# Sums of w_out's pieces by accumulating transfers, and a set of differences on GpSimd in place of VectorE

## The chip, the cores and the metric

The kernel runs on one core of one Trainium2 chip. The metric is the device time of one execution in microseconds; the time before is the median of three runs. The profiled execution is one more run of the same program. Engines are named as in the profile: PE (TensorE matmul), PEld (its weight loads), DVE (VectorE), ACT (ScalarE), POOL (GpSimd), SP (SyncE).

## The reference

Two blocks follow one another: a chunked state-space scan (mamba2 SSD) over x (4, 8, 768, 32), a, B and C, and a feed-forward layer with ELU on its result.

```python
for c in range(nc):                       # chunks of 32
    L = np.exp(cum[:, :, :, None] - cum[:, :, None, :]) * causal
    M = np.einsum('bhin,bhjn->bhij', Cc, Bc) * L
    y[:, :, sl] = M @ xc + (Cc @ state) * exp(cum)
    state = decay_full * state + sum_j(Bx * decay_from_j)
x = y.transpose(0, 2, 1, 3).reshape(B * S, H * D)      # (3072, 256)
h = x @ w_in                                           # (3072, 2048)
g = np.where(h > 0, h, np.exp(np.minimum(h, 0)) - 1)
out = g @ w_out                                        # (3072, 256)
```

All inputs and the output are float32, as the kernel sees them; the weights come as pairs of 32-bit words that the kernel first puts together.

## The kernel before, in words

The 3072 tokens are 12 blocks of 256, taken two at a time; a pair is named by its first block n = 0, 2, 4, 6, 8, 10. Each pair passes through the scan (`scores`, `sums`, `weigh`, `states`, `across`, `inside`), the first layer and the second layer. The order of the instructions of every engine is the order in which the program issues them (`tc.manual_schedule()`): no planner moves anything, and an engine that waits holds up all that stands behind it. The scan of pair n + 2 is woven into the first layer of pair n, and the second layer of pair n - 2 too.

**First layer.** For the columns m = 8 to 15 of pair 2 and for all columns of later pairs (m = 0 to 15, 128 columns each), `l1_words` splits each product into three passes of word products on PE (L791): the high words `w1` with `y1`, the low words `w0` with `y0`, and `both`. It needs, of the weights' piece i = m // 2, the tile `w_words` (`words_of_w`: an ACT copy L740 and a DVE operation L741) and the low words (`low_of_w`: two differences on POOL, shown at L851, because `sub` is there). After the products come ACT L799, DVE L802, ACT L808 and L809 (`begin_end`), then DVE L816 (`end_words`), which for even m is followed by a difference on POOL (L851 g<-g). `both_of_y` and `words_of_y` (L763, L766, L776) prepare the words of y for the next pair; PE needs them at the start of that pair's stage.

**Second layer.** For the first pair it is `l2`, direct products with `w_out` (L835). For later pairs `second` does it by blocks in seven products instead of eight (L910, a form of Strassen's): the weight matrix is cut in four, `a_out` = a11, a12, a21, a22, each 128 partitions x 8 x 128 as a strided view of `w_out`, and products r = 0 to 6 use a11, a12, s1, s2, s3, a22, s4. These sums of the weights are

- s3 = a11 - a21 (`s_out[1]`), s1 = a21 + a22 (over a21 itself), s2 = s1 - a11 (`s_out[0]`), s4 = a12 - s2 (`s_out[2]`).

They are made once, in 8 slices of 128x128. `differences` (POOL, L851 w_sum<-w_out) makes s3, since s1 overwrites a21. `sum_weights` (POOL, L718, three operations for each slice) makes s1, s2, s4 for slices 0 to 5 in the iterations j = 8 to 13, each after the last direct product that reads that slice of a21. The six operations for slices 6 and 7 (`left`) are handed to DVE, two in each of the iterations k = 2, 3, 4 of pair 4's stage. On the side of g, `quarters` gives b11, b21, b12, b22; `sum_t1` forms b12 - b11 and `sum_t2` forms t from b22 - b12. `sum_t1` of pair 2 is issued with `nc.vector` (DVE, L864), four times, at i = j - 8 = 0, 1, 3, 4.

Products and adds of the second layer alternate between two pools of PSUM: `ps_o` of even numbers comes from a pool with one buffer, so a product r + 2 waits until the adds of product r (DVE L888, ACT L922 and L947) have read it.

**Queues around the change.** Loads are issued by SP. POOL issues no transfer. On POOL, in j = 7, stand the two selects of a decay (L530), the low words of piece 5, then the scaling of B for blocks 4 and 5 (L412), then the weight sums. On ACT, in j = 6 and 7, stand the exponentials of the decays (L525), the copy of block 0's result (L841) and `elu`.

Of the kernel before, what the change touches and what calls it, by code (L numbers as in the profile page):

```python
# [14 lines left out]
ALU = mybir.AluOpType  # L15
ACT = mybir.ActivationFunctionType
# [16 lines left out]
def kernel(  # L33
# [27 lines left out]
    nc = tc.nc  # L61
# [30 lines left out]
    for k in range(4):  # L92
        (nc.scalar if k % 2 else nc.sync).dma_start(
            out=la0[BH * k:BH * (k + 1)],
            in_=a.rearrange("b h (c s) -> (b h) c s", s=P)[:, 0:2, :])
# [187 lines left out]
    for v in range(2):  # L283
        nc.gpsimd.affine_select(
            out=low16[Q * v:Q * v + Q], in_=low16[Q * v:Q * v + Q], pattern=[[1, Q]],
# [5 lines left out]
        out=hmask, in_=hmask, pattern=[[-N, NH]], compare_op=ALU.is_ge, fill=0.0,  # L291
        base=0, channel_multiplier=1)
    nc.gpsimd.affine_select(
        out=hmask, in_=hmask, pattern=[[N, NH]], compare_op=ALU.is_ge, fill=0.0,
# [8 lines left out]
        out=minus, in0=ident, scalar1=-1.0, scalar2=None, op0=ALU.mult)  # L303
# [213 lines left out]
    def decay(n, q):  # L517

        decay_of(n, 2 * q)
        decay_of(n, 2 * q + 1)  # L520
# [185 lines left out]

    def sum_weights(eng, a, s, i):
        for step in weight_steps(eng, a, s, i):  # L710
            step()

    def weight_steps(eng, a, s, i):
        a11, a12, a21, a22 = (part[:, i] for part in a)
        s2, _, s4 = (part[:, i] for part in s)
        for out, in0, in1, op in (
                (a21, a21, a22, ALU.add), (s2, a21, a11, ALU.subtract), (s4, a12, s2, ALU.subtract)):
            yield lambda: eng.tensor_tensor(out=out, in0=in0, in1=in1, op=op)  # L718

    def weight_sums():  # L720
        return [conv.tile([P, MC // 2, P], F32, tag="w64", name="w_sum", bufs=W_AHEAD)
                for _ in range(3)]

    w_parts = w_out.rearrange("p (i k) (r c) -> p k r i c", k=2, c=P)
    a_out = [w_parts[:, k, r] for r in range(2) for k in range(2)]
    s_out = []
# [8 lines left out]
    def words_of_w(i):  # L735

        w = pieces[i][0]
        k_words[i] = conv.tile(
            [P, 2, KC, CW], F32R, tag="w64", name="w_words", bufs=W_AHEAD)
        nc.scalar.activation(k_words[i][:, 0], w, ACT.Copy, scale=NEAR)  # L740
        nc.vector.scalar_tensor_tensor(  # L741
            out=k_words[i][:, 1], in0=k_words[i][:, 0].bitcast(F32), scalar=1.0 / WORD - 1.0,
            in1=w, op0=ALU.mult, op1=ALU.add)

    def low_of_w(i):

        w0 = conv.tile([P, KC, CW], F32R, tag="w_in", name="w0", bufs=DF // CW + 1)
        for k in range(KC):
            sub(w0[:, k], pieces[i][0][:, k], k_words[i][:, 0, k].bitcast(F32))
        k_words[i] = k_words[i], w0  # L750
# [99 lines left out]
    def sub(out, in0, in1):  # L850
        nc.gpsimd.tensor_tensor(out=out, in0=in0, in1=in1, op=ALU.subtract)  # L851

    def quarters(n, i):


        if n == 2 and i < DIRECT:
            A, B = g_of[n, i], g_of[n + 1, i]
            return A[:, 0], A[:, 1], B[:, 0], B[:, 1]
        A, B = g_of[n, 2 * i], g_of[n, 2 * i + 1]
        return A[:, 0], B[:, 0], A[:, 1], B[:, 1]  # L860

    def sum_t1(n, i, eng=nc.gpsimd):
        b11, b21, b12, b22 = quarters(n, i)
        eng.tensor_tensor(out=b12, in0=b12, in1=b11, op=ALU.subtract)  # L864
# [107 lines left out]
    def w_take(i, low):  # L972

        w_abs(i)
        w_low(i, low)
        w_sign(i)

    def w_give(i):

        w_high(i)  # L980
        w_sum(i)
# [190 lines left out]
            at = k // 2 * 2 + late  # L1172
            turn_part(*[(m, 0), (m, 1), (m, 2), (m + 1, 0), (m + 1, 1), (m + 1, 2), (m, 3), (m + 1, 3)][at])

    def differences(i, count):
        for r in range(i, i + count):
            sub(s_out[1][:, r], a_out[0][:, r], a_out[2][:, r])

    for j in range(2 * DIRECT):
        n, i = 2 + j // DIRECT, j % DIRECT  # L1180
        if j < 7:
            l2(0, j)
        piece = todo < len(pieces) and j != 1
        if j == 0:
            elu()
        if piece:
            w_take(todo, nc.vector)
        l1(n, i)
        if j == 7:
            l2(0, j)  # L1190
        if j == 0:
            scaled(3, nc.gpsimd)
            turn(3)
            elu()
            turn_exp(3)
        if piece:
            w_give(todo)
            todo += 1
        while lag:
            elu()  # L1200
        if j == 4:
            w_take(todo, nc.scalar)
            w_give(todo)
            todo += 1
        if j == 0:
            decay(3, 2)
            decay(3, 3)
        if j == 1:
            scores(3)
            sums(3)  # L1210
            for q in range(4):
                weigh(3, q)
        if j == 2:
            states(3)
        if j == 3:
            inside(across(3), 3)
        if j == 4:
            words_of_y(2)
        if j == 4:
            words_of_w(4)  # L1220
        if j == 5:
            low_of_w(4)
        if j == 5:
            both_of_y(2)
        scan_ahead(j)
        if j == 3:
            s_out[:] = weight_sums()
        if j == 7:
            words_of_w(5)
            low_of_w(5)  # L1230
    for j in range(8, 16):
        i = j - 8
        l1_words(2, j, between=4 if i == 7 else None)
        for p in ((), (6,), (), (7,), (0,), (1,), (2,), ())[i]:
            words_of_w(p)
        for p in ((), (), (6,), (7,), (0,), (), (), ())[i]:
            low_of_w(p)
        if i == 7:
            l2(1, 6)
            l2(1, 7)  # L1240
        begin_end()
        if i == 0:
            turn_part(5, 2)
            scaled(4, nc.gpsimd)
            scaled(5, nc.gpsimd)
        if i < 2:
            load_bc(i + 6)
            l2(1, i)
        if i == 2:
            l2(1, 2, half=0)  # L1250
            scores(4, 5)
            sums(4, 5)
            for q in range(4):
                weigh_two(4, q)
            l2(1, 2, half=1)
            states(4)
            states(5)
            turn_part(4, 3)
            turn_part(5, 3)
            for to in (6, 7):  # L1260
                load_b(to)
                spread_cum(to)
        if i == 3:
            l2(1, 3)
        if i == 4:
            y = across(4, 5)
            inside(y, 4, 5, ts=(0,))
            l2(1, 4)
        if i == 5:
            l2(1, 5, half=0)  # L1270
            inside(y, 4, 5, ts=(1,))
            l2(1, 5, half=1)
        if i in (0, 1, 3, 4):
            sum_t1(2, (0, 1, 3, 4).index(i), nc.vector)
        if i in (4, 6):
            turn_part(6, i // 2 - 2)
        if i in (0, 2, 3, 5):
            differences((0, 0, 2, 4, 0, 6)[i], 2)
        if i < 6:
            sum_weights(nc.gpsimd, a_out, s_out, i)  # L1280
    end_words()
    for p in (1, 2):
        low_of_w(p)
# [2 lines left out]
    low_of_w(3)  # L1286
    sum_t2(2, 0)
    sub(g_of[2, 14][:, 1], g_of[2, 14][:, 1], g_of[2, 14][:, 0])
    left = (step for i in (6, 7) for step in weight_steps(nc.vector, a_out, s_out, i))

    def stage_scan(n, k):

# [19 lines left out]
    for n in range(4, NP, 2):  # L1312
        m = n + 2 if n + 2 < NP else None
        steps = second(n - 2)

        def l2s(count):
            for _ in range(count):
                next(steps)

        for k in range(16):  # L1320
            l1_words(n, k, between=m if k == 15 else None)
            turn_step(n, k // 2 * 2 + 1, k % 2)
            if n == 4 and k == 0:
                decay(6, 1)
            if n == 4 and 1 < k < 5:
                for _ in range(2):
                    next(left)()
            if m:
                stage_scan(n, k)
            begin_end()  # L1330
            if k == 0 and n > 4:
                store(n - 4, 0)
                store(n - 4, 1)
            if not m:
                l2s(4 if k % 2 else 3)
                continue
            l2s((3 + (n == 4), 3 - (n == 4), 3, 3, 3, 3, 3, 3, 4, 5, 2, 2, 3, 1, 1, 0)[k])
            if k == 9:
                scores(m, m + 1)
                sums(m, m + 1)  # L1340
                for q in range(4):
                    weigh_two(m, q)
                l2s(2)
                states(m)
            if k == 10:
                states(m + 1)
            if k == 13:
                y = across(m, m + 1)
                inside(y, m, m + 1, ts=(0,))
                l2s(4)  # L1350
                inside(y, m, m + 1, ts=(1,))
        if m:
            l2s(4)
            both_of_y(m)
        end_words()
        for _ in steps:
            pass
    n = NP - 2
# [34 lines left out]
```

## Time and profile before

| | |
|---|---|
| median of 3 runs | 350.58 us (350.37 to 350.59) |
| profiled execution | 350.72 us |
| its span | 348.8 us |
| granted clock of TensorE | 0.999 |
| busy share PE, PEld, DVE, ACT, POOL | 98%, 86%, 74%, 67%, 63% |
| POOL: 18 sums L718 | 3.6 + 3.4 + 3.1 us |
| POOL: 8 differences w_sum L851 | 4.3 us |
| DVE: 6 sums L718 | 0.30 to 0.81 us each, 125.7 to 133.1 us |
| DVE: 4 first sums of t, L864 | 0.68 to 0.96 us each, 88.0 to 104.1 us |

How to read it: times inside the span are in microseconds from its start. A line such as "L910 PE MATMUL ps_o<-w_out,g 128*128 128x128" gives the source line, the engine, the operation, and what is written from what; "x4" counts instructions; a bracket with an arrow gives the idle time of the engine before the instruction and what ended it. Matmuls are pipelined, so a busy PE is not PE at its peak.

### The profile page before, as it was taken

Reading aid. Unit: us, or ns where it says so; the run is one execution under the profiler, and the core shown is the slowest. Engines: PE = TensorE matmul, PEld = TensorE weight load, DVE = VectorE, ACT = ScalarE, POOL = GpSimd, SP = SyncE. Lnnn points to the kernel's source line nnn. Section 1 sums busy time; section 2 is a strip of 40 time slices with the busy share of each in tenths; the row PEclk is TensorE's granted clock in tenths of the full one; section 3 lists DMA queues with packets and bytes.
Section 4 is the critical chain, followed back from the end, with each engine's and each line's share of the span. In section 5 each row is a group of like instructions: output and inputs, shape, how many; then the busy total and the mean of one; then the engine's idle time right before and its main releaser. Section 6 shows DMA issues by size and latency. Waiting matters only on the chain.

```text
span 348.8 us, 9876 instructions
## 1 busy us (share of the span) xinstructions
PE 340.7 (98%) x3878; PEld 298.3 (86%) x3878; DVE 258.5 (74%) x514; ACT 235.2 (67%) x538; POOL 219.4 (63%) x338
## 2 busy tenths in 40 slices
PE   8999999999999999999999999999999999999996
PEld 5669888888878788888999988998988999999996
DVE  3998989879987799875878775888675756665232
ACT  4789989599748789647699447699557566665000
POOL 5554554558999998964196864196854174455860
PEclk9999999999999999999999999999999999999999
DMA  8988988551360601080431070320000100001002
GB/s 148 238 217 181 309 187 226 123 93 43 65 137 2 131 22 31 7 156 12 103 64 32 8 158 6 95 44 2 2 0 5 62 0 3 0 0 43 22 0 62
DMA packets 72727, 26.49 MB, mean 76 GB/s; under 512 B 57768, under 2 KB 67560, under 8 KB 72680
## 3 DMA queue, kind: packets, MB, share of 16 engines
q1 hardware_dynamic: 70360, 25.60, 31.6%
q8 instruction: 30, 0.49, 0.6%
q10 hardware_dynamic: 2320, 0.26, 0.5%
q14 instruction: 17, 0.14, 0.1%
HBM read 22.51 MB, written 3.34 MB: 74 GB/s over the span
## 4 chain that ended last, share of the span: by engine, by line
PE 80%; DVE 7%; ACT 6%; SPq 2%; DMA 2%; issue 2%; POOL 0%; DVEq 0%; ACTq 0%; POOLq 0%
PE ps_o L910 32%; PE ps_h L791 16%; PE ps_h L671 11%; PE ps_w L791 8%; PE ps_o L835 6%; PE ps_y L638 2%; DVE ps_h L802 2%; DMA w<-in_moe_w_in_dram 2%; ACT e L809 1%; ACT e L808 1%; PE ps_g L545 1%; PE ps_y L620 1%; PE ps_st L575 1%; ACT e L799 1%; ACT L L525 1%
## 5 line engine op out<-in xcount | busy, mean ns | idle before, releaser
L910 PEld LDWEIGHTS ps_o<-w_out,g 128*128 128x128 f32 x640 | 78.6, 191 | 3.6 <-ACT p_sum L922 0.2
L910 PE MATMUL ps_o<-w_out,g 128*128 128x128 f32 x640 | 80.3, 275 | 0.0
L808 ACT ACTIVATE e<-ps_h 128x512 f32<-128x512 f32 x72 | 43.0, 597 | 53.5 <-DVE ps_h L802 53.5
L816 DVE SCALAR_TENSOR_TENSOR g<-e,ps_h 128x512 f32<-128x512 f32 x72 | 49.3, 685 | 30.6 <-ACT e L809 30.1
L851 POOL TENSOR_TENSOR g<-g 128x256 f32<-128x256 f32 x36 | 27.2, 757 | 57.2 <-DVE g L816 56.9
L802 DVE SCALAR_TENSOR_TENSOR ps_h<-ps_h,e 128x512 f32<-128x512 f32 x72 | 50.0, 695 | 13.9 <-ACT e L799 11.3
L799 ACT ACTIVATE e<-ps_w 128x512 f32<-128x512 f32 x72 | 42.2, 586 | 14.4 <-PE ps_w L791 14.3
L791 PE MATMUL ps_w<-y_both,w_words 128*128 128x512 f32 x144 | 51.2, 435 | 0.5 <-DVE y_both L776 0.4
L809 ACT ACTIVATE e<-e 128x512 f32<-128x512 f32 x72 | 45.5, 632 | 2.3
L671 PE MATMUL ps_h<-yT,w_in 128*128 128x256 f32 (+1 forms) x208 | 45.2, 368 | 1.3 <-POOL w_in L252 1.3
L791 PE MATMUL ps_h<-y,w_words 128*128 128x512 f32 x144 | 46.1, 401 | 0.1
L791 PE MATMUL ps_h<-y,w 128*128 128x512 f32 x144 | 44.6, 391 | 0.0
L671 PEld LDWEIGHTS ps_h<-yT,w_in 128*128 128x128 f32 x208 | 36.3, 190 | 7.4 <-POOL w_in L252 2.6
L525 ACT ACTIVATE L<-L,ncum 128x64 f32<-128x64 f32 x160 | 42.2, 336 | 0.2
L910 PE MATMUL ps_o<-w_sum,g 128*128 128x128 f32 x304 | 38.5, 275 | 0.9 <-DVE p_sum L888 0.7
L910 PEld LDWEIGHTS ps_o<-w_sum,g 128*128 128x128 f32 x304 | 37.0, 192 | 2.5 <-POOL g L851 0.9
L530 POOL TENSOR_SCALAR_AFFINE_SELECT L<-L 64x512 f32<-64x512 f32 x40 | 29.6, 741 | 11.0 <-ACT L L525 9.7
L791 PEld LDWEIGHTS ps_h<-y,w 128*128 128x128 f32 x144 | 27.0, 188 | 6.4
L851 POOL TENSOR_TENSOR g<-t,g 128x256 f32<-128x256 f32 x40 | 28.1, 736 | 5.8 <-PE ps_o L910 5.7
L791 PEld LDWEIGHTS ps_h<-y,w_words 128*128 128x128 f32 x144 | 26.5, 188 | 5.9 <-PE ps_w L791 0.5
L835 PE MATMUL ps_o<-w_out,g 128*128 128x256 f32 x128 | 30.9, 383 | 0.0
L851 POOL TENSOR_TENSOR t<-g 128x256 f32<-128x256 f32 x40 | 29.1, 759 | 0.3
(134 smaller groups left out, 540.4 us busy)
## 6 DMA issues: line engine op xcount, KB each, us to landing
L<-flat SPq DMA_DIRECT2D x20, 256.0 KB
w<-in_moe_w_out_dram SPq DMA_DIRECT2D x8, 512.0 KB
w<-in_moe_w_in_dram SPq DMA_DIRECT2D x7, 512.0 KB
xr<-in_x_dram SPq DMA_DIRECT2D x24, 128.0 KB
out_dram<-c_sum SPq DMA_DIRECT2D x9, 256.0 KB
bc<-in_B_dram SPq DMA_DIRECT2D x24, 64.0 KB
bc<-in_C_dram SPq DMA_DIRECT2D x22, 64.0 KB
ec<-flat_exp SPq DMA_DIRECT2D x10, 128.0 KB
```

The source lines that it names most:

```text
L525: nc.scalar.activation(L[:, h, u], L[:, h, u], ACT.Exp, bias=ncum[:, u, row:row + 1])
L530: nc.gpsimd.affine_select(out=part, in_=part, pattern=[[0, 4], [0, 2], [1, Q]], compare_op=ALU.is_ge, fill=0.0, base=0, channel_multiplier=-1)
L671: nc.tensor.matmul(out=ps[:, j, toks], lhsT=w_in[i][:, k, j * P:(j + 1) * P], rhs=yT[n // 2][:, k, n % 2].rearrange("p u i -> p (u i)")[:, ...
L791: nc.tensor.matmul(out=ps, lhsT=lhs[:, k], rhs=rhs[:, k], start=k == 0 and lhs is not w0, stop=k == KC - 1 and lhs is not w1)
L799: nc.scalar.activation(e, both, ACT.Copy, scale=WORD)
L802: nc.vector.scalar_tensor_tensor(out=high, in0=high, scalar=WORD - 1.0, in1=e, op0=ALU.mult, op1=ALU.add)
L808: nc.scalar.activation(e, high, ACT.Relu, scale=-1.0)
L809: nc.scalar.activation(e, e, ACT.Exp, scale=-1.0)
L816: nc.vector.scalar_tensor_tensor(out=g_of[n, m].rearrange("p b i -> p (b i)"), in0=e, scalar=1.0, in1=h, op0=ALU.subtract, op1=ALU.max)
L835: nc.tensor.matmul(out=o_of[n][:, ts], lhsT=g_of[n, j][:, m % 2, ts * P:(ts + 1) * P], rhs=w_out[:, m], start=(m == 0 and ts == 0), stop=( ...
L851: nc.gpsimd.tensor_tensor(out=out, in0=in0, in1=in1, op=ALU.subtract)
L910: nc.tensor.matmul(out=ps[:, ts], lhsT=b[:, ts * P:(ts + 1) * P], rhs=a[:, i], start=(i == chunk[0] and ts == 0), stop=(i == chunk[-1]), s ...
```

## The change

All sums of the weights are now made of negating copies on ACT (`less`) and transfers that add the source to what stands in the destination (`plus`, issued from POOL's queue): s3 = -a21, then + a11; s2 = -s3, then + a22; s4 = -s2, then + a12; and a21 + a22 in place, in two halves. Each step reads the one before, so ACT waits for the transfers and POOL for ACT. `less` of s3 stands in j = 6 behind the decay's exponentials, its `plus` in j = 7 ahead of the low words of piece 5. `less` of s2 is at the end of i = 2 (after `begin_end` of m = 10), its `plus` in i = 3, `less` of s4 in i = 5 behind the copies to yT, its `plus` in i = 6. The first half of a21 + a22 is issued in i = 5, the second after `sum_t2(2, 0)`. The six operations on DVE in pair 4's stage are gone. `sum_t1` of pair 2 is issued from POOL.

```diff
-    def sum_weights(eng, a, s, i):
...
-        for out, in0, in1, op in (
-                (a21, a21, a22, ALU.add), (s2, a21, a11, ALU.subtract), (s4, a12, s2, ALU.subtract)):
-            yield lambda: eng.tensor_tensor(out=out, in0=in0, in1=in1, op=op)
+    def less(out, in_):
+        nc.scalar.activation(out, in_, ACT.Copy, scale=-1.0)
+    def plus(out, in_, rows=slice(None)):
+        nc.gpsimd.dma_start(out=out[:, rows], in_=in_[:, rows], accum_op=ALU.add)
...
-    def differences(i, count):
-        for r in range(i, i + count):
-            sub(s_out[1][:, r], a_out[0][:, r], a_out[2][:, r])
...
+        if j == 6:
+            less(s_out[1], a_out[2])
         if j == 7:
             words_of_w(5)
+            plus(s_out[1], a_out[0])
             low_of_w(5)
...
         if i in (0, 1, 3, 4):
-            sum_t1(2, (0, 1, 3, 4).index(i), nc.vector)
+            sum_t1(2, (0, 1, 3, 4).index(i))
...
-        if i in (0, 2, 3, 5):
-            differences((0, 0, 2, 4, 0, 6)[i], 2)
-        if i < 6:
-            sum_weights(nc.gpsimd, a_out, s_out, i)
+        if i == 2:
+            less(s_out[0], s_out[1])
+        if i == 3:
+            plus(s_out[0], a_out[3])
+        if i == 5:
+            less(s_out[2], s_out[0])
+            plus(a_out[2], a_out[3], slice(0, 4))
+        if i == 6:
+            plus(s_out[2], a_out[1])
...
     sum_t2(2, 0)
     sub(g_of[2, 14][:, 1], g_of[2, 14][:, 1], g_of[2, 14][:, 0])
-    left = (step for i in (6, 7) for step in weight_steps(nc.vector, a_out, s_out, i))
+    plus(a_out[2], a_out[3], slice(4, 8))
...
-            if n == 4 and 1 < k < 5:
-                for _ in range(2):
-                    next(left)()
```

More of the change, by code (lines that the diff above doesn't have):

```diff
@@ L695, in elu @@
             op0=ALU.subtract, op1=ALU.max)
-    def sum_weights(eng, a, s, i):
[L710 to L715, printed above, removed]
-        for out, in0, in1, op in (
-                (a21, a21, a22, ALU.add), (s2, a21, a11, ALU.subtract), (s4, a12, s2, ALU.subtract)):
-            yield lambda: eng.tensor_tensor(out=out, in0=in0, in1=in1, op=op)
+    def less(out, in_):
+        nc.scalar.activation(out, in_, ACT.Copy, scale=-1.0)
+    def plus(out, in_, rows=slice(None)):
+        nc.gpsimd.dma_start(out=out[:, rows], in_=in_[:, rows], accum_op=ALU.add)
     def weight_sums():
```

## The prediction

> **What bounds the kernel now.** I read the busy shares first, then the table of stretches, the waits of the matmul engine, and at last the engines' timelines around the edited lines. A profiled execution took 350.72 us, of which the span is 348.8; the median of the three timed runs, 350.58, is 0.14 below it, so I build the sum on the profiled one and take 0.14 off.
>
> ```profile
> PE 340.7 (98%) x3878; PEld 298.3 (86%) x3878; DVE 258.5 (74%) x514; ACT 235.2 (67%) x538; POOL 219.4 (63%) x338
> ```
>
> PE has 8 us of idle in the whole span. The change touches 80 to 160 us. Columns of the stretches: window, length, then busy time of PE, PEld, DVE, ACT, POOL.
>
> ```profile
> 80.00:100.00 20.00, 19.56 (x251) 16.16 (x250) 18.84 (x39) 12.71 (x30) 18.51 (x31) 1.00 0.38 80
> 100.00:120.00 20.00, 19.50 (x234) 16.19 (x224) 15.89 (x24) 15.33 (x34) 19.22 (x28) 1.00 0.30 74
> 120.00:140.00 20.00, 19.13 (x124) 16.74 (x124) 18.55 (x33) 17.69 (x47) 18.42 (x26) 1.00 0.14 35
> 140.00:160.00 20.00, 19.43 (x347) 17.33 (x346) 15.41 (x37) 11.92 (x24) 14.20 (x26) 1.00 0.40 74
> 180.00:200.00 20.00, 20.00 (x256) 18.22 (x254) 15.41 (x32) 15.84 (x41) 15.59 (x23) 1.00 0.06 18
> ```
>
> Here POOL is busy 18 to 19 of 20 us and DVE up to 18.8, more than anywhere after; PE loses 2.4 us in the four stretches and nothing in the undisturbed one below. The waits of PE say on whom:
>
> ```profile
> PE ps_o L910 <- DVE p_sum L888: 0.7, 1, 0.7
> PE ps_st L575 <- DVE c_sum L888: 0.6, 1, 0.6
> PE ps_y L620 <- DVE g L816: 0.4, 1, 0.4
> PE ps_w L791 <- DVE y_both L776: 0.4, 1, 0.4
> PE ps_o L910 <- ACT c_sum L947: 0.2, 1, 0.2
> ```
>
> So PE is the bound, and behind it the DVE-ACT chain is just too late at five places. Idle is not all: the stage of pair 4 is also stretched where PE counts as busy. From the chain of waits, the third word product of a stage (k = 2) to its last (k = 15), first for pair 4, then for pair 6:
>
> ```profile
> 120.20 0.93 PE ps_h L791 x4
> 163.80 0.92 PE ps_h L791 x4
> 174.64 0.91 PE ps_h L791 x4
> 216.37 0.92 PE ps_h L791 x4
> ```
>
> 43.60 us against 41.73 for the same products: 1.87 us lost in the stage that holds the sums left to DVE. That is the most this stage can give back.
>
> **What the change removes.** POOL loses 8 differences (L851 w_sum, 4.3 us) and 18 sums (L718: 3.6 + 3.4 + 3.1), together 14.4 us between 91 and 116. DVE loses six sums in the stage of pair 4 (L718, 0.76 + 0.81 + 0.67 + 0.71 + 0.30 + 0.72 = 3.97 us, 125.7 to 133.1) and four first sums of t (L864, 0.95 + 0.85 + 0.68 + 0.96 = 3.44 us, 88.0 to 104.1).
>
> - In the stage of pair 4, the add for which PE waits runs at 130.10 behind 2.6 us of these sums; without them it is done before PE asks. I give the whole 1.87 back: **-1.87**.
> - The wait at L620 (0.44): DVE reaches that L816 at 98.68. Without two of the first sums (1.80 us before that point) and with POOL's Sx no longer held up (DVE stood 0.82 us on it at 96.75), it comes about 1 us earlier: **-0.44**.
>
> **What it adds.** Three negating copies of 128x1024 on ACT; by L922 (128x256, 0.35) and L799 (128x512, 0.59) each is 0.59 + 2 x 0.25 = 1.1 us. Four first sums of t on POOL, 4 x 0.76 = 3.0 us, in the place of 14.4. Five accumulating transfers, four issued where POOL's program still has work behind them that PE needs, three of 512 KB and two of half that. The trace has no transfer issued by POOL, so the time that an issue holds POOL (call it X) must be bounded.
>
> - Below: a load of SP's queue with as many pieces as ours (xr, 128 partitions x 8 heads, so 1024 runs) holds SP 0.47 to 0.58 us. Nothing lets it be below that, for it must write at least as many addresses.
> - Above: POOL summed the same 1024 runs in eight instructions of about 0.52 us, 4.2 us.
> - I take X = 3.0: it is POOL that works through the 1024 runs, as in its own row, while SP's row is that of a queue which computes nothing; nearer to POOL's.
>
> The first transfer is the one without cover. It stands in POOL's program behind the two selects of block 5's decay and ahead of the low words of piece 5, which PE uses in the third product of m = 10:
>
> ```profile
> 85.68 1.72 POOL L530 TENSOR_SCALAR_AFFINE_SELECT L<-L 64x512 f32<-64x512 f32 x2 [0.90 <-ACT L L525]
> 87.48 2.06 POOL L851 TENSOR_TENSOR w<-w_in,w_words 128x256 fp32r<-128x256 f32 x2
> 89.51 1.72 POOL L412 TENSOR_TENSOR b_tok<-b_tok,eb 128x256 f32<-128x256 f32 x2
> ```
> ```profile
> 89.39 0.63 PE L791 MATMUL ps_h<-y,w_words 128*128 128x512 f32 x2
> 89.86 0.62 PE L791 MATMUL ps_h<-y,w 128*128 128x512 f32 x2
> ```
>
> The low words end at 89.54; PE needs their second half at about 90.0. The cover is 0.5 us. The selects wait for ACT, where the first negation (1.1 us, less 0.17 of idle ahead of L841) now stands before the decay: they start at 86.6 and end near 88.2. Then X, then the two subtractions (1.4 to 2.06 us as here): they end at 89.6 + X to 90.3 + X. PE stands still for X - 0.4 to X + 0.3, about X - 0.1: **+2.9**. Behind them on POOL are b_tok (needed by PE at 92.40, L575; PE is late by then too, so nothing), one first sum, the difference of g for m = 8, and the next low words (needed at 103.7, covered by over 8 us).
>
> The second negation waits on ACT for the first transfer; ACT then sits idle for 4.18 us until 99.99 in the old trace, so it costs nothing unless the transfer lands more than 4 us late. Behind it on ACT stands L799 of m = 11.
>
> The second transfer is issued when POOL has done the difference of m = 10 (DVE's L816 near 98.4, counted without PE's stall), two low words and a first sum: from 101.3 to 104.3. The third negation, on ACT between the yT copies and L799 of m = 14, waits for its landing:
>
> ```profile
> 107.46 1.13 ACT L655 COPY yT<-ps_y 128x256 f32<-128x256 f32 x3
> 108.61 0.60 ACT L799 ACTIVATE e<-ps_w 128x512 f32<-128x512 f32 x1
> ```
>
> ACT, no longer behind DVE, ends the copies at 107.15. The last 64 KB store is issued by 346.6 and the span ends at 348.8, so a landing takes some 2.2 us; 512 KB at the page's highest rate (309 GB/s) take 1.7 us, twice that if the destination is read first, and all of it may pass during the issue. The landing is between 106.5 and 109.9; I take 108.0, 0.85 late. From there ACT's L759, DVE's L766 and L776 lead straight to PE's wait at 115.17. A punctual third negation would bring L759 to 110.8 instead of 111.14 (-0.35); 0.85 late makes it **+0.5**.
>
> The third and fourth transfers wait for PE (reads of the old piece, 106.7) and for ACT's third negation. Behind them are the low words of pieces 1 to 3, from 117.8 needed by PE one after the other; POOL has 14.4 - 3.0 = 11.4 us less to do there, which hides 1.5 X = 4.5. The fifth, half as large, holds the selects and the differences g<-t: their first is done at 126.3 today and used at 130.66, so about 2 us of cover after the 0.7 that PE wins; nothing at X/2 = 1.5, a wait beyond X = 4. PE's reads of the sums (from 123.9 on) come over 10 us after their issues.
>
> Sum: 2.9 - 1.87 - 0.44 + 0.5 = **+1.1 us**, 351.8 for a profiled execution, **351.7** for the median. Its own range is 351.3 (X = 2.6) to 354.0 (X = 4.2 and the second transfer 2 us late).
>
> **Rivals.**
>
> - *A short issue: faster.* If POOL's issue is like SP's, X = 0.6 to 1.2, the low words cost PE 0.5 to 1.1, the second transfer lands before 107, and the sum is 0.8 - 1.87 - 0.44 - 0.35 = -1.9: **348.7**. It decides below X = 2. For it: every row of a DMA issue in this trace without a full queue is under 0.6 us. Against it: none of those rows is POOL's. The Trainium skill, page "DMA: Bandwidth & Descriptors", section "Latency and other measured facts", puts the first byte of a transfer issued by GpSimd at about 1 us, the emission by its cores included, against 0.6 us for the other queues. By that figure X is 1 and the sum, as an estimate from that page, -1.8; no run shown here has such a transfer.
> - *Late landings: much slower.* The accumulation reads two operands for each one written, in runs of 512 bytes. If it lands 5 us after my 108.0, ACT waits as long and PE follows through y_both: +1.1 + 4 to 5, **356**. Against it: 512 KB of loads go by at over 200 GB/s in the first quarter.
> - *Even.* X near 2.4 with a punctual second transfer: 2.3 - 2.66 = -0.4, **350.2**. That the sums simply stay on POOL is no case: the program has five copies in their place.
>
> **Chances.** About 0.2%, 0.7 us, is what a measurement of this kernel can tell from no change. Forecast 0.39, late landings 0.10: slower 0.49. Short issue 0.39: faster. Even 0.12. The range takes the short issue down to X = 1 and the forecast up to the start of the late landings: 348.8 to 354.8; about 0.18 lies outside.
>
> **What would show it.** A gap of PE, some 3 us long at L791 of m = 10 with POOL's low words as its releaser, shows the first step; a gap of 1 us or less there means a short issue. The stage of pair 4 from k = 2 to k = 15 should take 41.7 us and its waits on L888 be gone; if it stays over 43, the gain was not DVE's sums. An idle ACT ahead of the third negation, released by a transfer, shows the second cost. I am wrong if POOL passes the first transfer in 1 us, or if PE idles for a transfer in the product with the sums.

## The result

The changed kernel takes 352.90 us, the median of 6 runs (352.18 to 354.42); the kernel before took 350.48 beside it (6 runs). The ratio is 1.0069, 95% interval 1.0046 to 1.0093: slower by 2.4 us. The profiled execution took 352.93 us, with a span of 351.0 and a granted clock of 0.995. Line numbers of the changed kernel, from the edited lines on, are those of before less 3 (L791 is now L788, L851 is L848, L816 is L813, L799 is L796); those ahead of them (L530, L575, L620) are the same. The negating copies are L711, the transfers L715.

### The profile page after: what moved, and what is told of

It reads as the page before. It is cut to its first block, busy times and chain, and to the rows that moved or that the text cites. A ratio compares the mean times of both kernels' runs of the same rounds, so it can differ in the third digit from the quotient of the medians.

```text
span 351.0 us, 9859 instructions
## 1 busy us (share of the span) xinstructions
PE 342.2 (97%) x3878; PEld 299.3 (85%) x3878; DVE 253.6 (72%) x504; ACT 237.7 (68%) x541; POOL 215.7 (61%) x321
## 4 chain that ended last, share of the span: by engine, by line
PE 84%; ACT 6%; DVE 2%; SPq 2%; DMA 2%; issue 1%; POOL 1%; ACTq 0%; POOLq 0%
PE ps_o L907 36%; PE ps_h L788 18%; PE ps_w L788 9%; PE ps_h L671 9%; PE ps_o L832 5%; PE ps_y L638 2%; ACT L L525 2%; DMA w<-in_moe_w_in_dram 2%; PE ps_g L545 2%; PE ps_y L620 1%; PE ps_st L575 1%; ACT e L684 1%; SPq L179 1%; DVE y L763 1%; ACT e L691 1%
## 5 line engine op out<-in xcount | busy, mean ns | idle before, releaser
L907 PEld LDWEIGHTS ps_o<-w_out,g 128*128 128x128 f32 x640 | 79.7, 194 | 3.4
L907 PE MATMUL ps_o<-w_out,g 128*128 128x128 f32 x640 | 81.3, 278 | 0.0
L813 DVE SCALAR_TENSOR_TENSOR g<-e,ps_h 128x512 f32<-128x512 f32 x72 | 49.3, 685 | 35.4 <-ACT e L806 35.0
L848 POOL TENSOR_TENSOR g<-g 128x256 f32<-128x256 f32 x36 | 27.4, 761 | 57.0 <-DVE g L813 56.6
L799 DVE SCALAR_TENSOR_TENSOR ps_h<-ps_h,e 128x512 f32<-128x512 f32 x72 | 50.0, 695 | 15.2 <-ACT e L796 12.6
L788 PE MATMUL ps_w<-y_both,w_words 128*128 128x512 f32 x144 | 51.8, 439 | 0.7 <-DVE y_both L773 0.6
L796 ACT ACTIVATE e<-ps_w 128x512 f32<-128x512 f32 x72 | 42.2, 586 | 13.7 <-PE ps_w L788 13.6
L671 PE MATMUL ps_h<-yT,w_in 128*128 128x256 f32 (+1 forms) x208 | 45.2, 368 | 1.9 <-POOL w_in L252 1.9
L788 PE MATMUL ps_h<-y,w 128*128 128x512 f32 x144 | 45.2, 393 | 1.7 <-DVE y L763 1.1
L788 PE MATMUL ps_h<-y,w_words 128*128 128x512 f32 x144 | 45.8, 399 | 0.1
L671 PEld LDWEIGHTS ps_h<-yT,w_in 128*128 128x128 f32 x208 | 36.3, 190 | 8.1 <-POOL w_in L252 3.4
L530 POOL TENSOR_SCALAR_AFFINE_SELECT L<-L 64x512 f32<-64x512 f32 x40 | 30.7, 767 | 10.6 <-ACT L L525 8.3
L788 PEld LDWEIGHTS ps_h<-y,w 128*128 128x128 f32 x144 | 27.0, 188 | 9.1 <-POOL w L848 3.1
L788 PEld LDWEIGHTS ps_h<-y,w_words 128*128 128x128 f32 x144 | 26.5, 189 | 6.1 <-ACT y L756 0.4
L848 POOL TENSOR_TENSOR g<-t,g 128x256 f32<-128x256 f32 x40 | 28.0, 734 | 5.8 <-PE ps_o L907 5.7
L848 POOL TENSOR_TENSOR t<-g 128x256 f32<-128x256 f32 x40 | 29.1, 757 | 0.3
```

What stands on the lines that cost most here:

```text
L530: nc.gpsimd.affine_select(out=part, in_=part, pattern=[[0, 4], [0, 2], [1, Q]], compare_op=ALU.is_ge, fill=0.0, base=0, channel_multiplier=-1)
L671: nc.tensor.matmul(out=ps[:, j, toks], lhsT=w_in[i][:, k, j * P:(j + 1) * P], rhs=yT[n // 2][:, k, n % 2].rearrange("p u i -> p (u i)")[:, ...
L788: nc.tensor.matmul(out=ps, lhsT=lhs[:, k], rhs=rhs[:, k], start=k == 0 and lhs is not w0, stop=k == KC - 1 and lhs is not w1)
L796: nc.scalar.activation(e, both, ACT.Copy, scale=WORD)
L799: nc.vector.scalar_tensor_tensor(out=high, in0=high, scalar=WORD - 1.0, in1=e, op0=ALU.mult, op1=ALU.add)
L813: nc.vector.scalar_tensor_tensor(out=g_of[n, m].rearrange("p b i -> p (b i)"), in0=e, scalar=1.0, in1=h, op0=ALU.subtract, op1=ALU.max)
```

## The profile after

The busy shares of the kernel after:

```profile
PE 342.2 (97%) x3878; PEld 299.3 (85%) x3878; DVE 253.6 (72%) x504; ACT 237.7 (68%) x541; POOL 215.7 (61%) x321
```

DVE and POOL both have less to do, as intended, and PE's busy time went up by 1.5 us for the same 3878 products. The stretches of the kernel after (window, length, busy time of PE, PEld, DVE, ACT, POOL, granted clock, DMA share, GB/s) show where:

```profile
80.00:100.00 20.00, 19.41 (x189) 15.49 (x188) 17.57 (x35) 15.24 (x35) 17.05 (x24) 1.00 0.51 94
100.00:120.00 20.00, 18.17 (x259) 13.93 (x258) 15.09 (x21) 12.77 (x25) 15.14 (x15) 0.99 0.90 134
120.00:140.00 20.00, 20.00 (x125) 18.17 (x125) 14.25 (x24) 18.67 (x50) 17.92 (x24) 0.93 0.35 63
140.00:160.00 20.00, 20.00 (x251) 18.02 (x249) 16.27 (x39) 12.36 (x26) 16.73 (x29) 1.00 0.37 72
```

In the second stretch PE is idle for 1.8 us, though no other engine is busy for more than 15.2 of 20; in the two after it it is never idle, but in the third the granted clock is 0.93. The waits of PE in the whole span without those of its start (L267 and L671), in total, number and longest:

```profile
PE ps_h L788 <- DVE y L763: 1.1, 2, 0.7
PE ps_h L788 <- POOL w L848: 0.6, 2, 0.4
PE ps_w L788 <- DVE y_both L773: 0.6, 1, 0.6
```

The waits on c_sum and p_sum in pair 4's stage are gone, and so is the one at L620. In their place are one of 0.6 us for POOL, and 1.7 us for the words of y, in the first column of pair 4.

Columns are followed best by their first product of the high words (`ps_h<-y,w_words` in PE's timeline; in most columns the two products of `both` stand ahead of it). That of m = 8 comes before PE meets anything that the edit changes, and lies between 82.0 and 84.1 us from one execution to the next. The table gives the start of each column's first such product after that point, in us, in each profiled execution. The kernels e1 to e9 are described below.

| | m=10 | m=11 | m=12 | m=14 | k=0 | k=1 | k=15 |
|---|---|---|---|---|---|---|---|
| before | 6.87 | 11.98 | 15.08 | 24.81 | 30.38 | 35.24 | 81.04 |
| after | 7.16 | 13.37 | 16.48 | 25.53 | 31.52 | 39.62 | 82.99 |
| e1 | 7.13 | 12.37 | 16.68 | 25.84 | 31.77 | 38.26 | 83.23 |
| e2 | 7.16 | 13.38 | 16.84 | 25.99 | 31.55 | 35.36 | 80.29 |
| e3 | 7.17 | 12.42 | 16.15 | 25.30 | 30.86 | 34.67 | 79.32 |
| e4 | 6.87 | 11.97 | 15.08 | 25.78 | 31.34 | 36.18 | 81.74 |
| e5 | 7.06 | 13.27 | 16.39 | 25.47 | 31.52 | 36.98 | 82.42 |
| e6 | 7.05 | 13.28 | 16.40 | 25.43 | 31.99 | 38.48 | 83.41 |
| e7 | 6.87 | 11.98 | 15.10 | 24.82 | 30.38 | 35.25 | 80.36 |
| e8 | 7.12 | 12.58 | 15.75 | 24.81 | 30.37 | 34.47 | 79.78 |
| e9 | 7.16 | 12.63 | 15.82 | 24.87 | 30.43 | 35.37 | 80.40 |

After against before, piece by piece: +0.3 to m = 10, +1.1 from m = 10 to 11, -0.7 from m = 12 to 14, +0.4 to k = 0, **+3.2 from k = 0 to 1**, and -2.4 in the rest of the stage; together +1.95 at k = 15. The first 0.3 arise ahead of m = 9. ACT's copy of block 0's result (L838) stands behind the first negation and ends at 84.96, and PE's next direct products start at 85.01; before, that copy ended at 83.49 and the products started at 84.09. The trace lists no wait there, and no run tests this cause.

**The first transfer.** All five transfers of the kernel after, then POOL's timeline around the first and PE's at m = 10 (start, length, engine, line, operation; the bracket is the idle time before and what ended it):

```profile
L715 POOL DMA_DIRECT2D w_sum<-w_out x3: 1544/1550/1768, 88.8 to 111.6; - x3
L715 POOL DMA_DIRECT2D w_out<-w_out x2: 1273/1848/2424, 107.5 to 127.6; - x2
DMA to landing us min/median/max: 4.2/6.4/8.9
```
```profile
87.13 1.72 POOL L530 TENSOR_SCALAR_AFFINE_SELECT L<-L 64x512 f32<-64x512 f32 x2 [1.57 <-ACT L L525]
88.81 1.77 POOL L715 DMA_DIRECT2D w_sum<-w_out  x1
90.65 1.42 POOL L848 TENSOR_TENSOR w<-w_in,w_words 128x256 fp32r<-128x256 f32 x2
```
```profile
90.42 0.63 PE L788 MATMUL ps_h<-y,w_words 128*128 128x512 f32 x2
91.43 0.49 PE L788 MATMUL ps_h<-y,w 128*128 128x512 f32 x1 [0.38 <-POOL w L848]
92.12 0.50 PE L788 MATMUL ps_h<-y,w 128*128 128x512 f32 x1 [0.20 <-POOL w L848]
```

An issue of 512 KB (the three that write w_sum) holds POOL for 1.5 to 1.8 us, and over all five transfers the data have landed 4 to 9 us after the issue. PE's two gaps are 0.6 us of waiting; with the slower start of each product the column loses 1.1.

**The second transfer and the third negation.** ACT's negations s2 and s4 in the kernel after, then DVE's preparation of the words of y and POOL beside it:

```profile
97.77 1.06 ACT L711 ACTIVATE w_sum<-w_sum 128x1024 f32<-128x1024 f32 x1 [2.29 <-DMA w_sum<-w_out]
110.21 1.06 ACT L711 ACTIVATE w_sum<-w_sum 128x1024 f32<-128x1024 f32 x1 [0.49 <-DMA w_sum<-w_out]
```
```profile
112.39 1.36 DVE L738 SCALAR_TENSOR_TENSOR w_words<-w_words,w_in 128x512 fp32r<-128x512 f32 x1
114.73 2.16 DVE L763 SCALAR_TENSOR_TENSOR y<-y,yT 128x512 fp32r<-128x512 f32 x2
116.82 1.81 DVE L773 SCALAR_TENSOR_TENSOR y_both<-y,yT 128x512 fp32r<-128x512 f32 x2
```
```profile
111.57 1.55 POOL L715 DMA_DIRECT2D w_sum<-w_out  x1 [1.69 <-ACT w_sum L711]
112.49 5.00 POOL L848 TENSOR_TENSOR w<-w_in,w_words 128x256 fp32r<-128x256 f32 x4
```

Two things stand in one chain. ACT waits 0.49 us for the second transfer and then negates for 1.06, ahead of L796 of m = 14 and of its own copy for y. And POOL, idle for 1.69 us because the fourth transfer has to wait for that negation, does the low words of pieces 1 and 2 only afterwards, just when DVE makes the words of y: DVE's L763 takes 2.16 us for two, its L773 1.81.

**The clock.** The two-microsecond stretches of the kernel after, with the granted clock third from the end:

```profile
114.00:116.00 2.00, 1.51 (x7) 0.71 (x5) 1.90 (x4) 1.34 (x3) 1.92 (x3) 1.00 1.31 144
116.00:118.00 2.00, 0.85 (x2) 0.25 (x2) 2.00 (x3) 0.00 (x0) 1.48 (x2) 1.00 1.24 198
118.00:120.00 2.00, 1.81 (x9) 1.46 (x10) 1.84 (x4) 0.13 (x1) 0.00 (x0) 0.87 0.76 198
120.00:122.00 2.00, 2.00 (x12) 2.00 (x11) 0.84 (x2) 1.97 (x5) 0.22 (x1) 0.50 1.01 164
122.00:124.00 2.00, 2.00 (x10) 1.65 (x9) 1.34 (x3) 2.00 (x9) 2.00 (x3) 0.78 0.49 79
```

PE was busy for 2.4 of the 4 us from 114 to 118. Then the granted clock reads 0.50 for a whole stretch and 0.87 and 0.78 in its neighbours, while PE shows no idle time from 120 us on. These two are means: with finer stretches the clock is 0.50 from 119.5 to 122.8 and 1.00 up to 119.4 and from 122.9. All six runs of the kernel after have a mean clock of 0.990 to 0.995. The Trainium skill, page "TensorE: Matmul & The Clock Gate", section "What's actually happening", has the clock go to half after an idle window of about 3.4 us that runs freely. The trace agrees in the half clock, but not in the idle window: PE was busy for 59% of the 4 us ahead.

**The stage of pair 4**, k = 2 and k = 15, in the chain of waits of the kernel after:

```profile
125.32 0.91 PE ps_h L788 x4
166.50 0.92 PE ps_h L788 x4
```

It takes 41.18 us, even less than the 41.73 forecast. The experiments show that the change's own gain here is smaller.

## The experiments

The first four kernels ran on one chip beside a median of 350.98 for before (31 runs), e5 to e8 on another beside 350.93 (31 runs), e9 beside 350.57 (17 runs). Each number is a median of 10 runs, 12 for e9. The theory at the start: the loss is made of PE's stall at m = 10 and of the late words of y, the first worth about 1 us and the second 2 to 3. The rival: the stall alone carries it, as the prediction had it.

**e1_low_words_first**: the first transfer goes behind the low words of piece 5.

```diff
             words_of_w(5)
-            plus(s_out[1], a_out[0])
             low_of_w(5)
+            plus(s_out[1], a_out[0])
```

> The first transfer issued behind the low words of piece 5 instead of ahead of them. Theory (the cost lies in where the issues and negations stand): PE's wait for POOL at m = 10, 1.1 us with the clock of the traces, goes, and nothing else: 351.8 us against 352.9 of the changed kernel. Rival A (the cost is the traffic of the transfers themselves, or the program as a whole): unchanged, 352.9.

Measured: 353.65 us, ratio 1.0069 (1.0047 to 1.0091), no gain at all; its profiled execution, at 352.02, is the fastest of its ten. The stall did go (m = 11 at 12.37 instead of 13.37), but at m = 12 nothing of it is left. A line of ACT's timeline and one of PE's waits in e1:

```profile
97.20 1.06 ACT L711 ACTIVATE w_sum<-w_sum 128x1024 f32<-128x1024 f32 x1 [2.88 <-DMA w_sum<-w_out]
```
```profile
PE ps_h L788 <- ACT e L796: 1.0, 1, 1.0
```

The first transfer now lands later, the second negation waits for it longer, and L796 of m = 11, behind it on ACT, keeps PE waiting for 1.0 us. So PE's wait for POOL hid a second wait of the same length.

**e2_s4_late**: the third negation moves behind the last direct products, past the words of y, and its transfer behind the low words of pieces 1 and 2.

```diff
             l2(1, 7)
+            less(s_out[2], s_out[0])
...
         if i == 5:
-            less(s_out[2], s_out[0])
             plus(a_out[2], a_out[3], slice(0, 4))
-        if i == 6:
-            plus(s_out[2], a_out[1])
...
     for p in (1, 2):
         low_of_w(p)
+    plus(s_out[2], a_out[1])
```

> The third negation on ACT moved out of the chain that makes the words of y for pair 4, to behind the copy of block 1's result, and its transfer behind the low words of pieces 1 and 2. Theory: the words of y come 1.1 to 1.5 us earlier, PE's idle ahead of pair 4's stage falls from about 3 us to 1 or less, and TensorE's granted clock stays at 1.00 between 118 and 124, which is worth 1.6 us more: 349.9 us, between 349.4 and 350.6. Rival B (the words of y are late because POOL's low words of pieces 1 and 2 now run beside DVE's operations on y and slow them down): the wait stays above 2 us and the clock still drops: 352 or more. Rival A: unchanged.

Measured: 350.07 us, ratio 0.9966 (0.9946 to 0.9986): 0.9 us below before, and 3.6 below after by the two ratios to before (0.0103 of 350.5). From k = 0 to 1 it needs 3.81 us instead of 8.10, and PE does not wait for the words of y. This is where the time had gone.

**e3_both_moves**: e1 and e2 together.

> Both moves. Theory: the gains add, 352.9 - 1.1 - 3.0 = 348.8 us, faster than the kernel before by some 1.7. Rival A: 352.9. Rival B: 351.8.

Measured: 349.51 us, ratio 0.9956 (0.9936 to 0.9975). The first move is worth 0.6 us on top of e2, half of what was expected, and the intervals overlap.

**e4_t_on_gpsimd_only**: the kernel before with only the second part of the change.

```diff
-            sum_t1(2, (0, 1, 3, 4).index(i), nc.vector)
+            sum_t1(2, (0, 1, 3, 4).index(i))
```

> The kernel before with the four first sums of t on POOL instead of DVE and nothing else changed. Theory: DVE is freed of 3.4 us between 88 and 104, but POOL, busy 92 to 96 per cent there, gets 3.0 us more and hands over its low words later: within 0.7 of 350.5 to slower by 1, and PE's wait at L620 (0.44) gets no shorter. Rival: that move alone is the gain, 349.8.

Measured: 352.16 us, ratio 1.0038 (1.0017 to 1.0060). By itself the move of the first sums of t costs 1.2 us. The waits of PE in e4:

```profile
PE ps_y L620 <- POOL Sx L597: 0.6, 1, 0.6
PE ps_y L620 <- DVE g L816: 0.4, 1, 0.4
```

With the sums of the weights still on POOL, its Sx comes too late, and the wait for DVE stays beside it.

**e5_s4_transfer_late_only**: of e2, only the transfer moves; the negation stays in i = 5.

```diff
-        if i == 6:
-            plus(s_out[2], a_out[1])
...
     for p in (1, 2):
         low_of_w(p)
+    plus(s_out[2], a_out[1])
```

> The changed kernel with the fourth transfer (s4 + a12) issued behind POOL's low words of pieces 1 and 2; the third negation stays on ACT where the change has it. POOL then makes those low words some 3 us earlier and no longer beside DVE's operations on y (L763, L773). Theory C (two causes of about equal size: ACT is 1.1 us late, and POOL's work beside DVE costs another 1.2): y_both comes 1.2 us earlier, PE's idle ahead of pair 4's stage is about half, the granted clock stays at 1.00: 351.0, between 350.5 and 351.6. Rival (ACT's lateness alone): no change in the wait, 352.5 to 353.5. Rival (POOL's work alone): as good as e2, 350.1.

Measured: 351.71 us, ratio 1.0022 (0.9996 to 1.0048), between after and e2. DVE and POOL in e5:

```profile
113.48 1.64 DVE L763 SCALAR_TENSOR_TENSOR y<-y,yT 128x512 fp32r<-128x512 f32 x2
115.04 1.28 DVE L773 SCALAR_TENSOR_TENSOR y_both<-y,yT 128x512 fp32r<-128x512 f32 x2
```
```profile
111.82 2.14 POOL L848 TENSOR_TENSOR w<-w_in,w_words 128x256 fp32r<-128x256 f32 x2 [2.35 <-issue]
113.91 1.56 POOL L715 DMA_DIRECT2D w_sum<-w_out  x1
```

Counted from m = 8, DVE's L773 is done at 32.59 in before (115.11), 35.37 in after (118.63), 34.32 in e5 (116.32) and 32.53 in e2 (115.49). So of 2.8 us, 1.05 go when POOL's low words move away from DVE, and 1.8 come with the negation in ACT's chain (in the latter 0.35 of the same contention, for e2's L763 pair takes 1.29 us and that of e5, beside a last subtraction, 1.64). The split is rough, for the negation waits 1.26 us for its transfer in e5 and 0.49 in after. The trace of after gives much the same: counted from m = 8, ACT's copy for y (L756) starts 1.80 us later than in before, and the other 0.98 are added behind it.

DVE's four operations take 2.92 us here, 3.97 in after and 2.58 in e2, where POOL is idle beside them. POOL works on a transfer's issue (113.91 to 115.47) beside the end of the L763 pair and the start of the L773 pair, which is not stretched; its subtractions do stretch them. So did the sums of the weights that POOL made there in the kernel before:

```profile
111.78 1.61 DVE L766 SCALAR_TENSOR_TENSOR y<-y,yT 128x512 fp32r<-128x512 f32 x2
113.31 1.80 DVE L776 SCALAR_TENSOR_TENSOR y_both<-y,yT 128x512 fp32r<-128x512 f32 x2
```

These make 3.41 us. The change thus did not bring this contention; it put other work of POOL's in the same place. The Trainium skill, page "SBUF — State Buffer", section "Who interferes with whom", says that a DVE instruction with two inputs in SBUF contends with one of GpSimd that reads SBUF. The trace agrees: the L773 pair takes 1.81 us beside subtractions in after and 1.29 beside an idle POOL in e2.

**e6_pe_kept_busy**: ten more products in PE's waits at the head of pair 4's stage, to tell the clock from the waits.

```diff
+            if (n, m) == (4, 0) and ps is both or (n, m) == (4, 0) and lhs is w0:
+                for _ in range(5):
+                    nc.tensor.matmul(out=both, lhsT=w1[:, 0], rhs=..., start=True, stop=True)
```

> The changed kernel with ten products more, of words of weights that lie in SBUF, put into PE's waits for the words of y at the start of pair 4's stage (their output is overwritten by the true product). Theory (the granted clock falls to a half after 118 because PE stood still for about half of 114 to 118): the clock stays at 1.00, the products cost some 0.4 us, and 1.1 to 1.6 us come back: 351.8. Rival (the clock falls for another reason, or costs nothing): 353.3 and the clock still below 1.00.

Measured: 353.13 us, ratio 1.0051 (1.0026 to 1.0075). The stretch that had a clock of 0.50 in after reads in e6:

```profile
120.00:122.00 2.00, 2.00 (x17) 1.88 (x16) 0.67 (x2) 1.59 (x3) 0.00 (x0) 1.00 0.97 177
```

The clock stays at 1.00 though the words of y are as late as in after (L773 is done 35.85 us from m = 8, there 35.37), and k = 0 to 1 takes 6.49 us instead of 8.10. But from k = 1 to 15 it takes 44.93 instead of 43.37: the waits on c_sum that had vanished from after are there again (0.6 at L575, 0.2 at L910). The likely reading is that the engines behind PE use its half clock to catch up, so that the drop costs far less than the 1.6 us seen at k = 1. But the ten products cost time of their own, and how much the drop costs is not settled: in e1 the four runs with a clock of 1.00 have a median of 353.0 and the six at 0.990 to 0.995 one of 354.3.

**e7_left_sums_on_gpsimd**: the kernel before, with the six operations of `left` issued from POOL instead of DVE.

```diff
-    left = (step for i in (6, 7) for step in weight_steps(nc.vector, a_out, s_out, i))
+    left = (step for i in (6, 7) for step in weight_steps(nc.gpsimd, a_out, s_out, i))
```

> The kernel before with the six sums of slices 6 and 7 on POOL instead of DVE, nothing else. By the prediction the stage of pair 4 from k = 2 to k = 15 gives back 1.87 us (41.7 instead of 43.5) and the kernel takes 349.1 on a scale where before takes 351.0. Theory from e2 and e3, whose stages still take 42.4 to 42.7: it gives back 0.9 to 1.1, 350.0. Rival: POOL, with 2.8 us more between 123 and 133, hands its differences to PE later and nothing is won.

Measured: 350.34 us, ratio 0.9975 (0.9952 to 0.9997), 0.6 us below before. From k = 2 to 15 it takes 42.83 us, where before took 43.52 by the same count: 0.7, not 1.87. The wait on p_sum at L910, 0.7 us in before, is the one that goes; those on c_sum at L575 and L910 stay.

**e8_first_transfer_early**: e2, and the first transfer goes up to j = 6, right behind its negation and ahead of the selects.

```diff
         if j == 6:
             less(s_out[1], a_out[2])
+            plus(s_out[1], a_out[0])
         if j == 7:
             words_of_w(5)
-            plus(s_out[1], a_out[0])
             low_of_w(5)
```

> e2 with the first transfer issued in j = 6 right behind its negation, ahead of the selects of block 5's second decay, where POOL stood idle for 1.6 us. Theory: neither the low words of piece 5 nor the second negation wait any longer for the first transfer, so both PE's stall for POOL at m = 10 and ACT's wait of 2 to 3 us go: m = 12 comes 15.4 us after m = 8 (e2: 16.84, e3: 16.15, before: 15.08), and the kernel takes 1.0 to 1.4 us less than e2, some 1.9 to 2.3 less than the kernel before. Rival (issuing is bounded by something else): as e3.

Measured: 349.17 us, ratio 0.9939 (0.9914 to 0.9963), the lowest ratio of all, though its interval overlaps that of e3: 1.8 us below before, 0.9 below e2. POOL's issue and ACT's second negation in e8:

```profile
84.35 1.77 POOL L715 DMA_DIRECT2D w_sum<-w_out  x1
```
```profile
94.43 1.05 ACT L711 ACTIVATE w_sum<-w_sum 128x1024 f32<-128x1024 f32 x1
```

The issue now takes POOL's idle time ahead of the selects, and the negation follows without a bracket, so without a wait. PE has no wait between 78 and 125 us. At k = 0 e8 stands where before does; its lead of 1.26 us at k = 15 is made from k = 0 to 1 (0.76; L773 is done at 31.83 instead of 32.59) and in the rest of the stage (0.5).

**e9_t_back_on_vector**: e8 with the four first sums of t on DVE again.

```diff
-            sum_t1(2, (0, 1, 3, 4).index(i))
+            sum_t1(2, (0, 1, 3, 4).index(i), nc.vector)
```

> The kernel e8_first_transfer_early with the four first sums of t of pair 2 on DVE again (the second part of the change undone in its best form). e4 showed those four sums to cost 1.2 us on POOL when POOL still made the sums of the weights. Theory: that cost was POOL's, busy 18 to 19 of 20 us there; in e8 POOL has the time (0.96 us of idle ahead of its L848 at 99.03) and DVE, which does L554, L592 and L448 without a gap from 93.14 to 98.3, has not. Then DVE's L813 of m = 10 comes up to 1.8 us later, PE waits at L617 again for 0.4 to 0.8 us, and the time is 0.3 to 0.8 us above that of e8: ratio to before about 0.995 to 0.9965. Rival: the four sums are better off on DVE in any case, as in e4; then it is about 1 us below e8, ratio 0.991, and no wait at L617 appears.

Measured: 350.27 us, ratio 0.9995 (0.9985 to 1.0004). Where POOL has the time, the sums of t on POOL are worth 1.1 us (by the medians) to 2.0 (by the ratios); where it had none (e4), they cost 1.2. The place was not the expected one: nothing waits at L620 (the expectation calls it L617). DVE's L760 of the words of y begins 29.32 us after m = 8 (111.80) instead of 28.41 in e8 (110.54), and k = 0 to 1 takes 4.94 us instead of 4.10. By k = 15 the two traces differ by 0.6 us; where the rest lies was not found.

## Why the prediction was right and wrong

The sign and the range were right, 352.9 against 351.7 in 348.8 to 354.8. The cause it gave was not: the stall that it blamed is worth about a third of its term, and the late negation that it put at 0.5 carries the loss. That the sum came within 1.2 us is in good part luck: one term was 1.8 too high, another 3.1 too low.

- **PE's stall, +2.9: measured +1.1.** The step that failed is the value of X: 3.0 us, "nearer to POOL's" row, where 1.77 was measured. The rest of that step held: the selects ended at 88.85 (forecast 88.2), the issue followed, then two subtractions, then PE; X - 0.1 would have been 1.7. By its own mark, a gap of 1 us or less, the first step was wrong and the short issue right. The rival's mechanism thus came true, X below 2, and its time did not. The page cited there, "DMA: Bandwidth & Descriptors" of the Trainium skill, gives about 1 us to the first byte; the runs show no first byte, but POOL is held for 1.77 us. PE itself came to this product 0.3 us later, which the prediction put at nothing. And e1 shows that this stall was not even the last to end: without it, PE waits behind the second negation.
- **The second negation, at nothing: a cover of 2.3 us, not 4.18.** The 4.18 us of idle named as its cover lie behind L799 of m = 11 in the old trace, which ran at 94.69, while the negation stands ahead of it. PE needs that L799 for m = 12, at 97.60, so the cover was 97.60 - 95.29 = 2.3 us, and waiting 2.29 and negating for 1.06 use up more than that. In after PE's own lateness hid it; in e1 it cost 1.0.
- **The stage of pair 4, -1.87: 0.7 in e7.** The term compared this stage with that of pair 6 and put the whole difference on the six sums, where only the wait on p_sum goes with them. The other kernels without them need 42.4 to 43.2 us from k = 2 to 15 (e1, e2, e3, e5, e6, e8, e9) against 43.52: 0.3 to 1.1. The 41.09 of after, below all of these, probably contain time that PE's lateness hands back.
- **The wait at L620, -0.44: gone, but not by the step named.** DVE's way from L554 to the L813 of m = 10 did become shorter, 5.15 us instead of 6.00, for POOL's Sx no longer holds it up. But L554, which needs PE's scores, began 1.25 us later behind the stall (11.41 us from m = 8 instead of 10.16), so L813 ended at 17.23, where before's L816 ended at 16.83. DVE is not early; PE, 1.4 late at m = 12, no longer meets it. The 0.7 us won from m = 12 to 14 are lateness handed back: in e8 and e9 too the wait is gone, and m = 14 starts no earlier than in before (24.81 and 24.87 against 24.81). Nor was the second part of the change needed for it: e9 has the first sums of t on DVE and no such wait, while e4, with that part alone, kept the wait and added another.
- **The late third negation, +0.5: measured +3.6**, the 0.4 before k = 0 and the 3.2 behind it. This is the step that decides. The mechanism was named, with ACT idle ahead of the negation and a transfer as releaser, and the wait of 0.49 us is even shorter than the 0.85 put down, though the transfer landed 1.5 us later than forecast (26.95 us from m = 8 against 25.48): ACT was late too. The size was wrong for three reasons. The term let ACT end the yT copies 1.44 us earlier than before (107.15 against 108.59), which would have paid for the negation. They began 0.4 later (25.33 us from m = 8 against 24.94), so the wait and the negation's 1.06 came on top, and ACT's copy for y came 1.8 later. Even in e8, with no stall and no negation there, that copy starts as in before (28.61 against 28.63): the 1.44 were not to be had. POOL's low words, said to be covered because POOL has 11.4 us less to do, were pushed behind the fourth transfer and ran beside DVE's words of y (1.05 us, e5). And behind the gap of PE that all this made the clock fell; what that costs in the end is open (e6).

The rival of late landings had the right place, the negation of s4 and y_both, with a wait of 5 us that did not come. e2 shows the change's idea to be sound: with the same five transfers and three negations, two of them moved, it is faster than before.

## What to carry to other kernels

When additions are replaced by transfers, cost the landing before the issue: here POOL was free after 1.8 us, and the next reader of the data had to wait 4 to 9. Issue each such transfer in the first idle gap after its source is ready, and keep the steps that wait for it off an engine's way to the next stage. Before moving work to an engine, look at what its own late work will then run beside: the same two subtractions were free at one place and stretched the critical operations of DVE at another.

## What was not expected of the hardware

- A transfer of 512 KB that adds to its destination, in runs of 512 bytes, holds POOL for 1.54 to 1.77 us and landed 6.4 to 8.9 us after its issue in the kernel after; with its two transfers of half the size the range is 4.2 to 8.9.
- Two operations of DVE with both inputs in SBUF take 1.28 to 1.29 us beside an idle POOL or one that issues a transfer (e2, e5), and 1.61 to 2.16 beside POOL's sums and subtractions (before, after).
- Behind 4 us in which PE was busy for 2.4, the granted clock was 0.50 for some 3.3 us in the kernel after; with ten more products in that gap (e6) it stayed at 1.00. But e1, with PE busy for 2.2 of the same 4 us in its profiled execution, kept 1.00 there too, so the busy share alone does not decide it.
